# Windowed attention and a sticky mixture of experts: local scores in 64-row by 32-column tiles, and half of v spread on the chip

## The chip, the cores and the metric

The kernel runs on one core of a Trainium2 chip. The metric is the device time of the program in microseconds; lower is better. A core has five engines that run their own instruction streams: TensorE (PE; PEld is its weight loading), VectorE (DVE), ScalarE (ACT), GpSimd (POOL) and SyncE (SP), which here issues most of the loads.

## The reference

There are 8 batches, 8 heads of 64 dimensions, 512 local and 32 global positions. A global query attends to everything; a local query attends to the 32 global keys and to local keys at most 32 positions away.

```python
k_all = np.concatenate([k_g, k_l], axis=2)
v_all = np.concatenate([v_g, v_l], axis=2)
out_g = np.matmul(sm(scale * np.matmul(q_g, k_all.transpose(0, 1, 3, 2))), v_all)
s_ll = scale * np.matmul(q_l, k_l.transpose(0, 1, 3, 2))
mask = np.abs(pos[:, None] - pos[None, :]) <= 32
s_ll = np.where(mask, s_ll, -1000000000.0)
s_lg = scale * np.matmul(q_l, k_g.transpose(0, 1, 3, 2))
a_l = sm(np.concatenate([s_lg, s_ll], axis=-1))
out_l = np.matmul(a_l, np.concatenate([v_g, v_l], axis=2))
x = np.concatenate([out_g, out_l], axis=2)   # then (B, S, H * D)
...
# per token: an expert is chosen (fresh, or the previous token's), then
h = np.maximum(x[b, s] @ w1[e], 0.0)
out[b, s] = p[e] * (h @ w2[e])
```

## The kernel before

The kernel has two stages. The attention (class Attn) works in units: per batch, four local units, one for each pair of heads, and two global units, one for two pairs. Their order is l0, l1, g0, l2, g1, l3; 48 units in all. Each batch also computes its gate logits (f1, f2, f3) and stores its rows to a scratch tensor in DRAM (f4). The experts (class Moe) then gather rows by expert and multiply them; their first pieces start during the last attention units.

The schedule is written out by hand in Attn.run. In step s it issues: the load of q and k two pairs ahead and of v one pair ahead (SP's queue); prep, which GpSimd does, for the next pair; the transposes of the probabilities of unit s - 2 (l_t, g_t); the mask matmul of unit s (l_m); a wide piece of the gate work; the scores of unit s (l_s, g_s) and their maximum (l_max, g_max); a thin piece; the exponential; and the product with v of unit s - 2 (l_av, g_av). Scores use a ring of three PSUM banks, the products a ring of two. Small steps of routing (the generators that drip calls) go between VectorE's instructions.

A pair's 512 queries are 16 windows of 32. The two heads lie on partitions 0 to 63 and 64 to 127 of the loaded tile raw. Before, prep copies q into a block-diagonal tile qbd (32 columns per head and window, the other head's half zero) and the keys into a tile kx, which for two windows holds their local blocks and the global block side by side. One matmul per window (L246) takes 64 columns of qbd as weights over all 128 partitions and streams 128 keys: 16 a pair. Each f32 matmul shows in the trace as two instructions, each with its weight load. Two windows share a bank column block, one on output partitions 0 to 63, one on 64 to 127. The mask is added first by a matmul with the identity (L235). VectorE takes the maximum (L251), subtracts it out of PSUM (L253), ScalarE applies the exponential (L257). After a transpose (L263) and a copy (L265) the product with v (L279) runs in 32-column tiles, and VectorE divides (L282, L284, L287).

v comes from DRAM already spread: for each of the 16 windows the 128 rows that its probabilities meet (its own, its neighbours' and the global ones), 16 x 130 columns, 1040 KB a pair. The host lays inputs out in _layout; no time is counted for it.

f4 stores a batch's 512 rows with one DMA (L420) from ScalarE's queue, for the last two batches from SP's. The first steps clear the zero halves of qbd and kx (blank).

## Time and profile before

| quantity | value |
|---|---|
| median of 3 runs | 682.33 us (679.4 to 682.5) |
| the profiled execution | 682.57 us |
| its span | 680.8 us |
| TensorE busy | 651.2 us |
| VectorE busy | 430.1 us |
| ScalarE busy | 344.6 us |
| GpSimd busy | 205.8 us |
| DMA moved | 151.46 MB |
| granted TensorE clock | 0.992 |

The span runs from the first to the last instruction; the time of an execution has 1.8 us around it. A row of a group has: line, engine, operation, output <- inputs by the program's names, shapes, xcount | busy us, mean ns of one | idle us of the engine just before them, and what ended that. A row of the timeline has: start us, duration us, engine, line, operation, xcount [idle before]. A row of the waits has: who, waited for whom: us in total, times, longest.

### The profile page before, as it was taken

Reading aid. Unit: us, or ns where it says so; the run is one execution under the profiler, and the core shown is the slowest. Engines: PE = TensorE matmul, PEld = TensorE weight load, DVE = VectorE, ACT = ScalarE, POOL = GpSimd, SP = SyncE. Lnnn points to the kernel's source line nnn. Section 1 sums busy time; section 2 is a strip of 40 time slices with the busy share of each in tenths; the row PEclk is TensorE's granted clock in tenths of the full one; section 3 lists DMA queues with packets and bytes.
Section 4 is the critical chain, followed back from the end, with each engine's and each line's share of the span. In section 5 each row is a group of like instructions: output and inputs, shape, how many; then the busy total and the mean of one; then the engine's idle time right before and its main releaser. Section 6 shows DMA issues by size and latency. Waiting matters only on the chain.

```text
span 680.8 us, 18547 instructions
## 1 busy us (share of the span) xinstructions
PE 651.2 (96%) x7261; PEld 560.6 (82%) x7261; DVE 430.1 (63%) x1090; ACT 344.6 (51%) x620; POOL 205.8 (30%) x342
## 2 busy tenths in 40 slices
PE   8899999998999999999999999999999999999994
PEld 6688788786776879887889888889898989898893
DVE  7878687787987877976407545526363627265552
ACT  4465665664555764555317626334455326166543
POOL 7644344343662310033012313040304020133113
PEclk9999999999999999989999999999999999999997
DMA  8857978879585596867318566437374626175583
GB/s 321 350 202 265 322 253 333 306 260 345 206 317 201 194 344 214 294 199 235 117 41 293 201 252 201 148 101 272 88 274 139 218 67 243 54 277 185 182 288 99
DMA packets 43013, 151.46 MB, mean 222 GB/s; under 512 B 7965, under 2 KB 9245, under 8 KB 38688
## 3 DMA queue, kind: packets, MB, share of 16 engines
q1 hardware_dynamic: 32080, 120.42, 50.5%
q0 software_dynamic: 6960, 21.90, 9.8%
q10 hardware_dynamic: 3744, 6.63, 2.6%
q8 instruction: 78, 1.28, 0.8%
q14 instruction: 151, 1.24, 0.6%
HBM read 130.55 MB, written 19.69 MB: 221 GB/s over the span
## 4 chain that ended last, share of the span: by engine, by line
PE 81%; DVE 10%; issue 4%; POOL 2%; ACT 1%; DMA 1%; POOLq 0%; ACTq 0%; DVEq 0%
PE ps L1284 27%; PE ps L1296 23%; PE ps L246 7%; PE ps L263 4%; PE ps L279 4%; PE ps L1238 3%; PE ps L1301 2%; PE ps L355 2%; DVE wp L1191 2%; PE ps L342 2%; PE ps L299 2%; PE ps L331 2%; PE ps L370 1%; DVE pe L253 1%; DVE mx L251 1%
## 5 line engine op out<-in xcount | busy, mean ns | idle before, releaser
L1312 POOL DMA_INDIRECT out_dram<-y,tk x39 | 41.3, 1058 | 311.8 <-ACT y L1309 155.4
L1284 PE MATMUL ps<-wp,wp 128*128 128x256 f32 (+6 forms) x744 | 118.0, 318 | 0.0
L1284 PEld LDWEIGHTS ps<-wp,wp 128*128 128x128 f32 x744 | 112.0, 189 | 5.4 <-ACT wp L1240 0.4
L1296 PE MATMUL ps<-wp,wq 128*128 128x512 f32 x444 | 111.5, 398 | 0.5 <-DVE wq L1288 0.5
L1296 PEld LDWEIGHTS ps<-wp,wq 128*128 128x128 f32 x444 | 81.6, 188 | 17.8 <-ACT wq L1286 0.7
L1288 DVE SCALAR_TENSOR_TENSOR wq<-ps,wq 128x384 fp32r<-128x384 f32 (+4 forms) x120 | 44.9, 409 | 55.9 <-ACT wq L1286 49.8
L1286 ACT ACTIVATE wq<-ps 128x256 fp32r<-128x256 f32 (+6 forms) x88 | 39.4, 452 | 72.7 <-PE ps L1284 65.8
L190 POOL TENSOR_SCALAR_AFFINE_SELECT qbd<-raw 64x512 f32<-64x512 f32 x62 | 44.3, 715 | 97.3 <-PE ps L246 89.0
L1241 DVE TENSOR_TENSOR wp<-ps,wp 128x512 fp32r<-128x512 f32 x40 | 27.6, 691 | 71.5 <-ACT wp L1240 71.3
L246 PE MATMUL ps<-kx,qbd 128*64 128x128 f32 x1024 | 64.7, 276 | 3.7 <-issue 3.6
L246 PEld LDWEIGHTS ps<-kx,qbd 128*64 128x64 f32 x1024 | 55.4, 137 | 11.7 <-issue 9.1
L251 DVE TENSOR_REDUCE mx<-ps 128x4 f32<-128x512 f32 x64 | 43.8, 685 | 30.0 <-PE ps L246 28.8
L1309 ACT ACTIVATE y<-ps,pp 128x512 f32<-128x512 f32 x39 | 26.8, 687 | 66.4 <-PE ps L1296 60.2
L257 ACT ACTIVATE pe<-pe 128x512 f32<-128x512 f32 x64 | 40.8, 638 | 37.9 <-DVE pe L253 37.9
L1191 DVE TENSOR_TENSOR wp<-raw,wp 128x1024 fp32r<-128x1024 f32 x47 | 56.7, 1218 | 4.5 <-ACT wp L1178 4.3
L1224 POOL DMA_INDIRECT xa<-xs,idx x42 | 50.5, 1203 | 17.3 <-issue 11.1
L1240 ACT CAST wp<-ps 128x512 fp32r<-128x512 f32 x40 | 23.3, 586 | 55.5 <-PE ps L1238 55.5
L1178 ACT CAST wp<-raw 128x1024 fp32r<-128x1024 f32 x49 | 50.6, 1047 | 0.9 <-PE ps L342 0.6
L253 DVE TENSOR_TENSOR pe<-ps,mx 128x512 f32<-128x512 f32 x64 | 43.9, 686 | 1.0
L190 POOL TENSOR_SCALAR_AFFINE_SELECT kx<-raw 128x384 f32<-128x384 f32 (+3 forms) x127 | 42.8, 370 | 2.7 <-DMA raw<-in_qk_dram 0.6
L279 PEld LDWEIGHTS ps<-v,pt 128*32 128x32 f32 x2048 | 32.1, 110 | 11.4 <-issue 8.8
L265 ACT COPY pt<-ps 128x512 f32<-128x512 f32 x64 | 34.7, 599 | 10.8 <-PE ps L263 10.8
(284 smaller groups left out, 1183.0 us busy)
## 6 DMA issues: line engine op xcount, KB each, us to landing
raw<-in_w_dram SPq DMA_DIRECT2D x78, 512.0 KB
v<-in_vw_dram SPq DMA_DIRECT2D x32, 1040.0 KB
raw<-in_qk_dram SPq DMA_DIRECT2D x32, 528.0 KB
xa<-in_w_dram SPq DMA_DIRECT2D x26, 512.0 KB
xT<-in_w_dram SPq DMA_DIRECT2D x20, 512.0 KB
xs<-xa ACTq DMA_DIRECT2D x6, 1056.0 KB
xs<-xa SPq DMA_DIRECT2D x2, 1056.0 KB
qgb<-in_qg_dram SPq DMA_DIRECT2D x8, 128.0 KB
```

The source lines that it names most:

```text
L190: self.nc.gpsimd.affine_select(out=out, in_=in_, pattern=pat, compare_op=ALU.is_ge, fill=0.0, base=0, channel_multiplier=0)
L246: nc.tensor.matmul(sp[64 * t2:64 * t2 + 64, t], qbd[:, w], kf[:, f:f + P], start=False, stop=True, skip_group_check=True)
L251: nc.vector.tensor_reduce(out=mx, in_=st["sps"][hb], axis=AX.X, op=ALU.max)
L253: nc.vector.tensor_tensor(out=st["pe"][:, 4 * hb:4 * hb + 4], in0=st["sps"][hb], in1=mx.broadcast_to([P, 4, P]), op=ALU.subtract)
L279: nc.tensor.matmul(o[32 * w4:32 * w4 + 32, g, h], pt[:, 2 * g + w4 // 2, w4 % 2, h, :], v[:, w, h * (D + 1):(h + 1) * (D + 1)], start=True ...
L1178: (nc.vector.tensor_copy if dve else nc.scalar.copy)(out=hi, in_=raw)
L1191: (nc.gpsimd if pool else nc.vector).tensor_tensor(out=lo[:, f], in0=raw[:, f], in1=hi[:, f].bitcast(F32), op=ALU.subtract)
L1224: self.nc.gpsimd.indirect_dma_start(out=self.xr[j] if k == "early" else self.xr4[:, j], out_offset=None, in_=src, in_offset=bass.IndirectO ...
L1284: nc.tensor.matmul(ph, a[:, dc, fs], b_[:, dc, n0:n1], start=(n == 0), stop=(n == 11))
L1288: nc.vector.scalar_tensor_tensor(out=t, in0=ph[:, a - n0:b_ - n0], scalar=0.0, in1=hh[:, fc, a:b_].bitcast(F32), op0=ALU.max, op1=ALU.subt ...
L1296: nc.tensor.matmul(py, a[:, fc, js], b_[:, fs], start=(fc == 0 and k == 0), stop=(fc == 7 and k == 2))
L1312: sc = nc.gpsimd.indirect_dma_start(out=self.out, out_offset=bass.IndirectOffsetOnAxis(ap=self.g[1][:, j:j + 1], axis=0), in_=y, in_offset ...
```

## The change

- q is used as it lies. For each window and head one matmul takes 32 columns of q on that head's 64 partitions as weights and streams 128 keys on the same 64 partitions: 32 matmuls a pair on tiles of 64 rows by 32 columns, in place of 16 on 128 by 64. Scores of head h go to bank h. The mask is now two matmuls of 128 columns for each bank.
- k is loaded in blocks of 64 in an order PO, and prep writes one region of 28 blocks of 32 behind it, in the same tile: the global block, spread 14 times, and the local blocks 1 to 14. A pair's window reads two stretches of 64. qbd, kx and the clearing are gone.
- v is loaded for the eight even windows only (8 x 130 columns). The odd ones, which need the same rows except one neighbour, are written by GpSimd in two copies (prepv): 96 partitions x 1040, and 32 partitions x 910 from partitions 0 to 31 to 96 to 127.
- Each load of q and k or of v waits on SP until the last but one has landed (AHEAD = 2).
- A batch's row store is split in two; for the first six batches the second half is issued a step later, after the first exponential.
- The thin gate piece runs after the first product (after g_av, where there is none). The global scores are cut into 320 and 224 columns, with three exponentials in place of five.
- Buffers move: raw is wider, and the experts' row buffers xr, their output ring y and one weight buffer now lie in raw's upper part.

```diff
-GCH = [1, 4, 7, 10, 13, 14]
+GCH = [8, 2, 11, 5, 14, 0]
+PO = [0, 2, 3, 5, 6, 1, 4, 7]
+AHEAD = 2
...
+    def get(self, out, in_):
+        d = self.nc.sync.dma_start(out, in_)
+        if len(self.sent) >= AHEAD:
+            self.tc.add_manual_dep(d.ins, self.sent[-AHEAD].ins.name, mybir.DependencyInfo(mybir.DependencyClass.Sync, mybir.DependencyReason.DATA), reason="chain")
+        self.sent.append(d)
...
-        self.nc.sync.dma_start(t, self.qk[b, pr])
+        self.get(t[:, 0:33 * 32], self.qk[b, pr])
...
-        self.nc.sync.dma_start(v.rearrange("p w c -> p (w c)"), self.vw[b, pr])
+        self.get(v[:, 0:8].rearrange("p w c -> p (w c)"), self.vw[b, pr])
...
     def prep(self, u):
...
-            self.cp(qbd[0:64, :, 0, :], q[0:64], [[0, NW], [0, 32]])
-            self.cp(qbd[64:128, :, 1, :], q[64:128], [[0, NW], [0, 32]])
-        self.cp(kf[:, 1:5]...
-        self.cp(kf[:, 6:24]...
-        self.cp(kf[:, 24]...
-            self.cp(kx[:, 1:8, 2, :]...
+            self.cp(x[:, :, 0], g, [[0, 14], [0, 32]])
+            self.cp(x[:, :, 1], k[:, 1:15], [[0, 14], [0, 32]])
...
+    def prepv(self, u):
+        b, pr = u["u"]
+        v = self.cur[b]["v"][pr]
+        self.cp(v[0:96, 8:16], v[0:96, 0:8], [[0, 8], [0, VW]])
+        self.cp(v[96:128, 8:15], v[0:32, 1:8], [[0, 7], [0, VW]])
...
+        for sp in st["sps"]:
+            so = sp.rearrange("p t (k c) -> p t k c", c=32)
+            for par, mo in enumerate((so[:, 0:2, 1::2, :], so[:, 2:4, 0::3, :])):
+                nc.tensor.matmul(mo, self.cst.idb, self.mask[:, par], start=(par == 0), stop=False, skip_group_check=True)
...
-        for t in range(4):
-            for t2 in range(2):
-                w = 8 * hb + 2 * t + t2
-                f = 32 * (3 * (w // 2) + w % 2)
-                nc.tensor.matmul(sp[64 * t2:64 * t2 + 64, t], qbd[:, w], kf[:, f:f + P], start=False, stop=True, skip_group_check=True)
+        for t2 in range(2):
+            for par in range(2):
+                for w4 in range(4):
+                    for h in range(2):
+                        m = 4 * t2 + w4
+                        far = min(max(2 * m - 1, 1), 14) if par == 0 else min(2 * m + 2, 14)
+                        u0, u1 = 8 + PO.index(m), 16 + 2 * PO.index(far // 2) + far % 2
+                        d = slice(64 * h, 64 * h + 64)
+                        w = 2 * m + par
+                        nc.tensor.matmul(st["sps"][h][32 * w4:32 * w4 + 32, 2 * par + t2], q[d, 32 * w:32 * w + 32], ku[d, u0:u1 + 1:u1 - u0],
+                                         start=False, stop=True, skip_group_check=True)
...
-        q.dma_start(self.xs[r0:r0 + 4 * P].rearrange("(t p) r -> p t r", p=P), xa)
+        q.dma_start(out[:, 0:2], xa[:, 0:2])
+        if b < B - 2:
+            self.rows.append((out[:, 2:4], xa[:, 2:4]))
+        else:
+            q.dma_start(out[:, 2:4], xa[:, 2:4])
...
+                self.prepv(nx)
...
-                self.l_s(nx, 0)
+                self.l_s(nx)
                 self.l_max(nx, 0)
-                self.l_s(nx, 1)
                 self.l_max(nx, 1)
...
-            fpiece(thin)
             if nl:
                 self.l_exp(nx, 0)
             else:
                 self.g_exp(nx)
+            for _ in range(old):
+                nc.scalar.dma_start(*self.rows.pop(0))
             if sl:
                 self.l_av(st, 0)
+                fpiece(thin)
                 self.l_av(st, 1)
...
-        self.xr = [buf.tile([P, ROW], F32, name=f"xr{j}") for j in range(2)]
+        self.xr = [raw.t[j][:, 1024:1024 + ROW] for j in range(2)]
...
-    raw = ring(buf, [P, 32 * 33], F32, "raw", 4)
+    raw = ring(buf, [P, 1536 + ROW], F32, "raw", 4)
```

## The prediction

> **What bounds the kernel now.** I read the page first: the busy shares, the chain that ended last and the costliest groups.

> ```profile
> span 680.8 us, 18547 instructions
> PE 651.2 (96%) x7261; PEld 560.6 (82%) x7261; DVE 430.1 (63%) x1090; ACT 344.6 (51%) x620; POOL 205.8 (30%) x342
> PE 81%; DVE 10%; issue 4%; POOL 2%; ACT 1%; DMA 1%; POOLq 0%; ACTq 0%; DVEq 0%
> L246 PE MATMUL ps<-kx,qbd 128*64 128x128 f32 x1024 | 64.7, 276 | 3.7 <-issue 3.6
> ```

> TensorE is busy 96% of the span and 81% of the chain. The local scores (L246) are 64.7 us of that, so a microsecond off TensorE there is a microsecond off the end until another engine is in the way. Next I cut the attention into stretches of one batch's length (six units) by the windows view. Its columns are stretch, length, busy us of each engine, clock, DMA share, GB/s.

> ```profile
> 23.30:51.20 27.90, 25.55 (x586) 20.92 (x585) 21.86 (x85) 15.63 (x38) 12.48 (x28) 1.00 0.66 247
> 78.80:104.60 25.80, 25.71 (x590) 21.41 (x589) 21.32 (x73) 15.68 (x36) 11.03 (x24) 1.00 0.83 290
> 104.60:130.80 26.20, 25.85 (x589) 21.40 (x587) 20.94 (x73) 15.87 (x38) 11.05 (x24) 1.00 0.86 303
> 158.00:189.40 31.40, 28.91 (x616) 23.27 (x615) 25.87 (x91) 14.51 (x32) 16.59 (x33) 1.00 0.69 247
> 189.40:224.00 34.60, 31.77 (x656) 25.57 (x655) 26.82 (x99) 20.99 (x49) 15.94 (x29) 1.00 0.76 275
> 224.00:320.00 96.00, 91.66 (x773) 78.94 (x772) 76.69 (x191) 55.90 (x88) 21.41 (x23) 0.98 0.74 243
> ```

> A middle batch is TensorE alone: 25.71 of 25.80 us busy, at full clock. But VectorE is busy 21.32 of the same 25.80, and DMA 83 to 86%. After 224 us come the experts, which the change touches only by where buffers lie. Last, the timeline of two units, to see who waits for whom.

> ```profile
> 104.56 0.38 PE L235 MATMUL ps<-mask,idb 128*128 128x256 bf16 x2
> 105.31 1.97 PE L246 MATMUL ps<-kx,qbd 128*64 128x128 f32 x32
> 106.45 0.69 DVE L251 TENSOR_REDUCE mx<-ps 128x4 f32<-128x512 f32 x1 [1.84 <-PE ps L246]
> 107.17 0.69 DVE L253 TENSOR_TENSOR pe<-ps,mx 128x512 f32<-128x512 f32 x1
> 107.20 1.12 PE L279 MATMUL ps<-v,pt 128*32 128x65 f32 x64
> 108.26 0.88 PE L331 MATMUL ps<-idf,pg 128*128 128x128 f32 x6
> 108.97 0.38 PE L235 MATMUL ps<-mask,idb 128*128 128x256 bf16 x2
> 110.14 0.15 DVE L282 TENSOR_SCALAR rs<-ps 128x4 f32<-128x4 f32 x1
> 110.32 0.18 DVE L284 RECIPROCAL rs<-rs 128x4 f32<-128x4 f32 x1
> 110.54 0.42 DVE L287 TENSOR_TENSOR xa<-ps,rs 128x256 f32<-128x256 f32 x1
> DVE mx L251 <- PE ps L246: 27.7, 21, 2.2
> L279 PE MATMUL ps<-v,pt 128*32 128x65 f32 x2048 | 37.7, 221 | 2.3 <-issue 1.5 <-DVE rv L894 0.3 <-DVE xa L287 0.2
> ```

> TensorE goes from one group to the next without a hole. VectorE is the one that waits, for the first half of the scores, 1.3 us each time (27.7 over 21 waits).

> **The local scores, the main term.** Before, a pair's scores are 32 passes (16 f32 matmuls, two instructions each) on 128-row by 64-column tiles; two such tiles stand side by side. 32 passes take 1.97 us, a single one 0.276, so they start (1.97 - 0.276) / 31 = 54.6 ns apart. With two tiles running together that is 109 ns per pass on a tile, 0.85 ns a column. L279 shows the same with four 32-column tiles: (1.12 - 0.221) / 63 = 14.3 ns apart, 57 ns per pass on a tile, 0.88 ns for each of 65 columns. So column tiles overlap in full, twofold and fourfold, both passes of a matmul included.

> After, there are 64 passes of 128 columns on eight tiles (two row halves, one per head, by four column strips). Nothing in this trace runs a row-split tile. If all eight overlap, starts are 109 / 8 = 13.7 ns apart and the block takes 63 x 13.7 + 276 = 1.14 us: 0.83 us saved a pair, 26.6 us over 32 pairs. If only the four column strips overlap, starts are 27.3 ns apart and the block takes 1.99 us: nothing gained. If neither did better than the present 54.6 ns, the block would take 3.7 us: a loss of 56 us. I take 13.7 ns, since L279 already issues at 14.3 with as many columns open and the two heads write different banks.

> [...]

> **Mask.** Four matmuls of 128 columns replace two of 256.

> ```profile
> 9.12 0.27 PE L235 MATMUL ps<-mask,idb 128*128 128x256 bf16 x1 [1.40 <-DVE pe L253]
> L1023 PE MATMUL ps<-oe,o x21: 167/168/182, 201.8 to 202.5; 128*128 128x12 bf16 x21
> ```

> The two of 256 at 104.56 come 0.38 less the 0.27 of a single one, 0.11 us, apart, 0.22 a pair. L1023 issues 21 bf16 matmuls, with full weights, in 0.7 us, 33 ns each, so 55 ns for half the columns is not held up by the weights. I take 0; the other end, 0.11 us for each of four, is +0.22 x 32 = 7 us.

> **VectorE, who is late next.** A batch needs 25.71 - 4 x 0.83 = 22.4 us of TensorE against VectorE's 21.3. Also, scores now come by head, both banks complete only at the block's end, so the first reduction no longer starts halfway. VectorE's work for a unit after that end is four operations of 0.69 and two evacuations of about 0.75 (0.15, 0.18 and 0.42), 4.24 us. The unit that starts at 104.56 lasts 4.41 to the next mask and would last 3.58: a deficit of 0.66 us. Units beside global ones have slack and catch up. TensorE needs the first bank back for the mask after 1.12 of L279 and 0.88 of L331, 2.0 us from the block's end; VectorE frees it after 1.4, so some 0.6 us of lag costs nothing. I take 0.8 us a batch, 6.4 in all; the ends are 0 and half of what was saved (1.7 a batch, 13 us).

> **GpSimd.** Rows of its copies, all at L190:

> ```profile
> L190 POOL TENSOR_SCALAR_AFFINE_SELECT qbd<-raw 64x512 f32<-64x512 f32 x62 | 44.3, 715 | 97.3 <-PE ps L246 89.0 <-DMA raw<-in_qk_dram 4.1 <-DMA xr<-xs,idx 2.1
> L190 POOL TENSOR_SCALAR_AFFINE_SELECT kx<-raw 128x384 f32<-128x384 f32 x32 | 17.8, 555 | 0.0
> L190 POOL TENSOR_SCALAR_AFFINE_SELECT kx<-raw 128x224 f32<-128x224 f32 x31 | 12.9, 416 | 0.0
> L190 POOL TENSOR_SCALAR_AFFINE_SELECT kx<-raw 128x128 f32<-128x128 f32 x32 | 9.5, 295 | 2.7 <-DMA raw<-in_qk_dram 0.6
> L190 POOL TENSOR_SCALAR_AFFINE_SELECT kx<-raw 128x32 f32<-128x32 f32 x32 | 6.9, 214 | 0.0
> ```

> A pair costs 2 x 0.715 + 0.555 + 0.416 + 0.295 + 0.214 = 2.91 us. After: two key copies of 448 columns, 0.555 + 64 x 0.87 ns = 0.61 each; two v copies of 1040 and 910 columns, at 1.09 ns a column (715 - 295 over 384) 1.29 and 1.15; together 3.66. A batch rises from 11.0 to 14.0 us of 23, and GpSimd was waiting for TensorE for 89 us, so this is hidden: 0. Behind the v copy, which waits for its load, stand the next pair's key copies, the setup and ranking steps and the gathers; scores and products that need the copies come two units later. If the v copies ran at half that speed GpSimd would need 24 us a batch and set the pace, at +1 us a batch or 8 in all.

> **Loads and stores.**

> ```profile
> v<-in_vw_dram SPq DMA_DIRECT2D x32, 1040.0 KB
> raw<-in_qk_dram SPq DMA_DIRECT2D x32, 528.0 KB
> 121.76 0.37 ACTq L420 DMA_DIRECT2D xs<-xa  x1
> ```

> v drops from 1040 to 520 KB a pair: 32 x 520 KB, 16.6 MB less. A middle batch moves 290 GB/s x 25.8 us = 7.5 MB; it would move 5.4 in 23.2, 232 GB/s, a share near 0.66. Each load waits on SP for the last but one; behind it on SP stand the query loads, the global rows' stores and at the end the weight loads; GpSimd waits for those loads. 303 GB/s at a share of 0.86 is 352 at full share, 1.5 us a load; a pair's two loads have 5.8 us. I take 0. Six half stores more on ScalarE (15.9 of 26.2 us busy) and two fewer exponentials a global unit are hidden by its slack; the thin pieces, moved behind the first exponential and product, feed work one unit later: 0. Uncovered they would cost at most a store issue each, 6 x 0.4 us.

> **Supply of instructions.** TensorE also stands still where the profile shows no wait:

> ```profile
> q8 instruction: 78, 1.28, 0.8%
> 32.03 0.87 PE L246 MATMUL ps<-kx,qbd 128*64 128x128 f32 x11 [1.64 <-issue]
> 77.53 0.43 PE L342 MATMUL ps<-v,ptg 128*32 128x65 f32 x16 [1.50 <-issue]
> 165.81 0.76 PE L246 MATMUL ps<-kx,qbd 128*64 128x128 f32 x9 [1.95 <-issue]
> ```

> These fall in stretches with heavy loads, and instructions arrive by DMA too. The change eases the loads but adds 32 matmul and 32 weight-load instructions a pair. I take 0, between -5 (these three gone) and the loss of the third rival.

> **Start.** The clearing of block-diagonal buffers goes from VectorE, so the wait of 1.40 us at 9.12 can; the first v copies then queue on GpSimd ahead of the next keys. 0, between -1.4 and +2.

> Sum: 682.6 (the profiled execution, 680.8 of span and 1.8 around it; 0.2 over the median 682.33) - 26.6 + 6.4 = 662.4 us.

> **The rivals.** First, VectorE or GpSimd takes back half or more of the gain: 26.6 - 13 - 8 leaves 6 us, 26.6 - 13 leaves 14; 669 to 677, centre 673. For it speaks VectorE at 21.3 against 22.4, against it the 0.6 us of lag that is free. [...]

> Second, the row halves do not overlap, and the change does not do what it says: blocks of 1.99 us, 683, with the mask's end up to 690. For it: no row-split tile is in the trace. Against: strips overlap without loss.

> Third, slower: TensorE runs out of instructions. A batch now executes 590 + 589 in 25.8 us, 45.7 a us. After, it has 4 x 64 more and 16 for the masks, 1451, in 23.2 us, 62.5 a us. Below 1451 / 25.8 = 56 a us the batch is slower than before; at 54 it takes 26.9, 1.1 us more, 691. For it the holes above; against it the lower DMA share, and 128 instructions in L279's 1.12 us.

> Fourth, more is gained: no VectorE loss, the three holes and the 1.4 at the start gone: 682.6 - 26.6 - 5.1 - 1.4 = 649.5.

> **How the numbers follow.** Likeliest (652 to 669) 0.56; VectorE or GpSimd 0.13; the floor 0.03; no overlap 0.10; supply 0.10; more gained 0.08. A change of 0.5%, 3.4 us, is about what a measurement of this kernel can tell. Faster: 0.56 + 0.13 + 0.03 + 0.08 = 0.80, less 0.01 for the edge of the floor: 0.79. No overlap splits into 0.06 same and 0.04 slower; with the edge, same 0.07; slower 0.10 + 0.04 = 0.14. The range 650 to 682 leaves out the supply case, most of no overlap and part of the last.

> **What would show it.** L246's successor: 64 matmuls in 1.1 to 1.2 us, right; near 2.0, the second rival. A batch of 23 to 24 us with VectorE over 0.9 busy: right. Waits of TensorE's mask or products for L253 and L287 above 1 us a batch: the first rival; issue holes above the present ones: the third. DMA share near 0.66, GpSimd 14 us a batch. What makes the prediction wrong is mainly the untested row split, then the supply.

## The result: 1.1% slower, and where the profile shows it

The changed kernel takes 687.97 us (median of 4 runs, 687.05 to 689.35), the kernel before beside it 680.87 us (4 runs, 679.36 to 682.5): a ratio of 1.0106, interval 1.0069 to 1.0142. The forecast was 662 us and faster.

The profiled executions are 687.05 us now and 682.57 before, so they show 4.5 of the 7.1 us between the medians. All of it lies in the attention: its last score block ends at 224.1 us before and at 229.3 us after, and what follows takes 456.7 and 456.1 us. The page of the changed kernel, the lines that answer to those shown of before:

```profile
span 685.3 us, 20668 instructions
PE 633.9 (92%) x8349; PEld 540.1 (79%) x8349; DVE 431.8 (63%) x1087; ACT 337.7 (49%) x588; POOL 225.1 (33%) x279
q8 instruction: 85, 1.39, 0.8%
L251 PE MATMUL ps<-raw 64*32 64x128 f32 x2048 | 41.5, 282 | 8.8 <-issue 8.6
L200 POOL TENSOR_SCALAR_AFFINE_SELECT v<-v 96x1040 f32<-96x1040 f32 x64 | 66.9, 1045 | 51.4 <-DMA v<-in_vw_dram 31.2
v<-in_vw_dram SPq DMA_DIRECT2D x32, 520.0 KB
```

TensorE lost 17.3 us of busy time (651.2 to 633.9) and the span grew all the same: work went and idle time came. The score row went from 64.7 to 41.5 us of busy time, its idle time from 3.7 to 8.8, and nearly all of that is "issue", time with no wait that the profile shows. The same stretches as before (stretch, length, busy us of each engine, clock, DMA share, GB/s), and one of 3.5 us:

```profile
23.30:51.20 27.90, 23.82 (x715) 18.59 (x713) 20.73 (x79) 14.21 (x31) 16.70 (x20) 0.94 0.55 169
78.80:104.60 25.80, 22.63 (x710) 17.93 (x689) 23.06 (x72) 13.85 (x31) 13.36 (x16) 1.00 0.67 214
104.60:130.80 26.20, 22.18 (x664) 17.50 (x661) 20.07 (x65) 14.23 (x32) 11.24 (x14) 0.93 0.66 211
111.50:115.00 3.50, 3.50 (x110) 2.94 (x100) 1.95 (x5) 0.21 (x1) 3.15 (x4) 0.52 0.57 191
158.00:189.40 31.40, 27.02 (x796) 21.69 (x788) 25.99 (x90) 16.52 (x37) 11.46 (x15) 1.00 0.62 199
```

The DMA share has fallen to 0.66 as forecast, but TensorE is now idle for 3 to 4 us of each 26. The clock column, 1.00 in these stretches before, reads 0.94 and 0.93 in two of them: TensorE ran at half clock for a while. The row from 111.50 is one such piece, clock 0.52. The timeline (start, length, engine, instruction, and in brackets the idle time before it and what ended it) shows a good unit and the two kinds of hole:

```profile
104.37 0.39 PE L236 MATMUL ps<-mask,idb 128*128 128x128 bf16 x4
...
105.13 1.16 PE L251 MATMUL ps<-raw 64*32 64x128 f32 x64
106.21 1.12 PE L285 MATMUL ps<-v,pt 128*32 128x65 f32 x64
106.32 0.69 DVE L257 TENSOR_REDUCE mx<-ps 128x4 f32<-128x512 f32 x1 [1.86 <-PE ps L251]
...
108.14 2.15 POOL L200 TENSOR_SCALAR_AFFINE_SELECT v<-v 96x1040 f32<-96x1040 f32 x2 [5.18 <-PE ps L334]
108.25 1.04 DVE L755 TENSOR_TENSOR leq<-L,lm 128x40 f32<-128x40 f32 x1
108.74 0.41 PE L251 MATMUL ps<-raw 64*32 64x128 f32 x5
...
111.35 1.74 PE L251 MATMUL ps<-raw 64*32 64x128 f32 x59 [2.20 <-issue]
...
166.46 2.15 POOL L200 TENSOR_SCALAR_AFFINE_SELECT v<-v 96x1040 f32<-96x1040 f32 x2 [6.00 <-PE ps L334]
167.72 0.91 DVE L765 TENSOR_TENSOR lvm<-sk,lvm 128x5 f32<-128x5 f32 x1
...
170.86 0.90 PE L345 MATMUL ps<-v,ptg 128*32 128x65 f32 x48 [2.63 <-DVE rs L288]
```

At 105.13 a score block takes 1.16 us: this part works. At 108.74 a block gets 5 passes out, stands still for 2.20 us with nothing to wait for, and does the other 59 at half clock (1.74 us). At 166.46 two v copies run on GpSimd; beside them VectorE takes 0.91 us for 5 columns, and then TensorE waits 2.63 us for VectorE. The view of waits over the attention (0 to 224 us; idle us of the waiting engine, number, longest) names the same two. It also names an engine, GpSimd, that waits for loads; from 5 us on, no hole of TensorE over 0.2 us in this trace ends with GpSimd:

```profile
POOL v L200 <- DMA v<-in_vw_dram: 31.2, 19, 4.9
POOL raw L200 <- DMA raw<-in_qk_dram: 29.4, 16, 5.3
PEld ps L251 <- issue: 14.8, 32, 2.5
PE ps L251 <- issue: 8.5, 5, 2.2
PE ps L345 <- DVE rs L288: 6.6, 4, 2.6
```

**An account of the attention.** For each kernel I took the holes of more than 0.2 us in TensorE (neither a matmul nor a weight load running; a wait for a semaphore that TensorE's queue records as an instruction of its own counts as hole) from 5 us to the end of the last score block, and sorted them by what ended them. A hole is "instruction" when the next instruction starts 0.9 to 1.7 us after a 16 KB packet of the instruction queue (q8 above) has landed and no engine has just released it. All holes counted so lie at one place of TensorE's stream: 193 or, seldom, 194 instructions past a multiple of 256, in the order of the trace. A hole is VectorE's, ScalarE's or GpSimd's when the next instruction, or the queue's wait just ahead of it, waits on a semaphore of that engine and starts 28 to 105 ns after an instruction of that engine ended. "Half" is the time at clock 0.5, which always came behind a hole, in pieces of 3.4 us or of two or three times that. "Work" is the end, less the holes, less half of "half"; that last term is an estimate, since TensorE need not have been the bound all through such a piece. Worked out from the traces, in us (number of instruction holes in brackets):

```
kernel                       end    instr.     VectorE ScalarE GpSimd other half  work
before                       224.1   7.5 (8)     1.9    1.0    0      1.5    0    212.1
after                        229.3  14.2 (12)   16.8    1.5    0      0.4  10.2   191.3
e1_no_chain                  241.7  25.2 (15)   14.9    1.0    0      0.8  17.1   191.2
e2_chain_one                 265.8   3.8 (4)    42.2    0.5    8.5    2.0  51.2   183.1
e3_small_copies              231.3  14.4 (14)   13.4    0.9    1.4    0.4  20.5   190.5
e4_whole_v                   250.1  33.0 (23)    8.2    1.4    0      3.2  27.3   190.6
e5_scores_alone              244.6  34.0 (23)    7.2    0.5    0      0    23.9   190.9
e6_after_more_instr          287.3  51.1 (30)    3.5    1.0    0      0    41.0   211.3
e7_before_more_instr         269.9  37.7 (23)    0.5    1.3    0      0    13.7   223.7
e8_small_loads               221.7   2.2 (3)    23.4    1.3    0      0    10.2   189.7
e9_half_loads                220.6  10.7 (15)   14.7    0.8    0      0     0     194.4
e10_small_loads_no_copies    207.4   1.6 (2)    12.1    1.3    0      0     3.4   190.7
e11_half_loads_small_copies  225.7   9.9 (11)   14.6    3.6    0.7    0    13.7   190.0
e12_quarter_loads            232.3  11.2 (14)   16.7    5.2    0      0    10.2   194.1
e13_copy_on_scalar           229.4   7.6 (8)    15.6   12.7    0      0     3.4   191.9
e14_half_loads_four          225.4   9.9 (14)   17.1    4.7    0      0     6.8   190.2
e15_before_part_loads        232.0   0.9 (1)     2.1   16.3    0.4    0    10.2   207.1
```

From before to after: work -20.8; VectorE's holes +14.9; instruction holes +6.7; half clock +5.1; ScalarE +0.5; other -1.1. That is +5.3, and the trace has +5.2.

Of VectorE's 16.8 us, 10.8 are in front of product matmuls (L345 6.9, L285 3.9; 0.5 before). They wait for a bank of the ring of two that VectorE empties by its division (L288, L290, L293): 9.3 of the 10.8 us end within 0.15 us of the end of L293. The mask, which waits for a score bank, has 2.5 us (1.4 before). A hole of 0.96 us that ends at 93.82 shows how VectorE comes late:

```profile
91.13 2.15 POOL L200 TENSOR_SCALAR_AFFINE_SELECT v<-v 96x1040 f32<-96x1040 f32 x2 [0.91 <-DMA v<-in_vw_dram]
92.24 0.18 DVE L290 RECIPROCAL rs<-rs 128x4 f32<-128x4 f32 x1
92.45 0.84 DVE L791 TENSOR_TENSOR gx<-lpr,lsu 32x8 f32<-32x8 f32 x1
93.33 0.42 DVE L293 TENSOR_TENSOR xa<-ps,rs 128x256 f32<-128x256 f32 x1
```

A routing step (L791) stands between two steps of the division. Beside the v copies it takes 0.84 us, 0.16 where no copy runs, and the product's bank comes free that much later.

Each row of the table is one profiled execution. Its time can lie several us from the median of its kernel: e7 8.0 us below, e13 3.6, e2 3.4 and e9 3.1 below, e1 2.9 above; e8 and e10 ran once. So differences of a few us between rows are not told apart by them. The expectations below were written with a count that took the recorded waits of TensorE's queue for work; in it VectorE's holes are 13.6 us in the changed kernel, 16.5 in e8 and 14.1 in e9.

### The profile page after: what moved, and what is told of

The parts are those of the page before. It is cut to its first block, busy times and chain, and to the rows that moved or that the text cites. A ratio compares the mean times of both kernels' runs of the same rounds, so it can differ in the third digit from the quotient of the medians.

```text
span 685.3 us, 20668 instructions
## 1 busy us (share of the span) xinstructions
PE 633.9 (92%) x8349; PEld 540.1 (79%) x8349; DVE 431.8 (63%) x1087; ACT 337.7 (49%) x588; POOL 225.1 (33%) x279
## 4 chain that ended last, share of the span: by engine, by line
PE 56%; DVE 5%; issue 2%; ACT 1%; POOL 0%; POOLq 0%; ACTq 0%; DVEq 0%
PE ps L1298 27%; PE ps L1310 23%; PE ps L1252 2%; PE ps L1315 2%; DVE wp L1205 1%; DVE wq L1205 1%; DVE hl L1302 0%; DVE xT L1021 0%; PE ps L1036 0%; POOL xa L1238 0%; DVE o L937 0%; DVE xl L1255 0%; DVE xT L1023 0%; PE ps L358 0%; POOLq L1460 0%
## 5 line engine op out<-in xcount | busy, mean ns | idle before, releaser
L1326 POOL DMA_INDIRECT out_dram<-raw,tk x39 | 41.1, 1053 | 311.0 <-ACT raw L1323 168.0
L200 POOL TENSOR_SCALAR_AFFINE_SELECT v<-v 96x1040 f32<-96x1040 f32 x64 | 66.9, 1045 | 51.4 <-DMA v<-in_vw_dram 31.2
L1323 ACT ACTIVATE raw<-ps,pp 128x512 f32<-128x512 f32 x39 | 26.8, 688 | 66.8 <-PE ps L1310 60.6
L1238 POOL DMA_INDIRECT xa<-xs,idx x42 | 51.0, 1214 | 16.7 <-issue 10.9
L285 PEld LDWEIGHTS ps<-v,pt 128*32 128x32 f32 x2048 | 33.5, 109 | 21.4 <-issue 10.2
L251 PE MATMUL ps<-raw 64*32 64x128 f32 x2048 | 41.5, 282 | 8.8 <-issue 8.6
L285 PE MATMUL ps<-v,pt 128*32 128x65 f32 x2048 | 41.1, 222 | 8.8 <-issue 3.7
L200 POOL TENSOR_SCALAR_AFFINE_SELECT raw<-raw 128x448 f32<-128x448 f32 x62 | 39.0, 655 | 30.1 <-DMA raw<-in_qk_dram 29.4
L251 PEld LDWEIGHTS ps<-raw 64*32 64x32 f32 x2048 | 30.4, 109 | 16.3 <-issue 15.5
## 6 DMA issues: line engine op xcount, KB each, us to landing
raw<-in_qk_dram SPq DMA_DIRECT2D x32, 528.0 KB
xs<-xa ACTq DMA_DIRECT2D x12, 528.0 KB
xs<-xa SPq DMA_DIRECT2D x4, 528.0 KB
```

Source lines behind the costliest of these rows:

```text
L200: self.nc.gpsimd.affine_select(out=out, in_=in_, pattern=pat, compare_op=ALU.is_ge, fill=0.0, base=0, channel_multiplier=0)
L251: nc.tensor.matmul(st["sps"][h][32 * w4:32 * w4 + 32, 2 * par + t2], q[d, 32 * w:32 * w + 32], ku[d, u0:u1 + 1:u1 - u0], start=False, stop ...
L285: nc.tensor.matmul(o[32 * w4:32 * w4 + 32, g, h], st["pts"][h][:, 2 * par + hb, c0:c0 + 32], v[:, 8 * par + m, h * (D + 1):(h + 1) * (D + ...
L1238: self.nc.gpsimd.indirect_dma_start(out=self.xr[j] if k == "early" else self.xr4[:, j], out_offset=None, in_=src, in_offset=bass.IndirectO ...
L1326: sc = nc.gpsimd.indirect_dma_start(out=self.out, out_offset=bass.IndirectOffsetOnAxis(ap=self.g[1][:, j:j + 1], axis=0), in_=y, in_offset ...
```

## The experiments

Four theories of what gave the gain back are tested; the letters are those of the expectations. S: the supply of instructions, TensorE waits for a fetch that stands behind data loads. C: the chain, a load that waits for the last but one comes late. G: GpSimd's v copies slow VectorE down. V: VectorE itself is late, by its own work. Ratios are against the kernel before on the same chip.

**The chain of loads.** First without it, then tighter.

```diff
-AHEAD = 2
+AHEAD = 99        # e1_no_chain
+AHEAD = 1         # e2_chain_one
```

> Only the chain is taken out: loads no longer wait for the last but one. Theory S (TensorE runs out of instructions, because there are more of them per microsecond and their fetch waits behind loads): bursts of loads come back, fetches wait longer, the holes with no wait grow from about 21 us; 690 to 696 us. Theory C (the chain makes loads late: GpSimd waited 61 us for DMA): these waits shrink below 20 us and 4 to 8 us come back; 680 to 684. Theory G (GpSimd's v copies hold VectorE's small two-input operations): no change, 686 to 690.

697.58 us, ratio 1.0213 (1.0141 to 1.0286), against 1.0106 (1.0069 to 1.0142) with the chain: slower, though the intervals touch. Its waits over the attention:

```profile
POOL v L200 <- DMA v<-in_vw_dram: 52.6, 18, 5.1
PE ps L251 <- issue: 11.3, 7, 2.6
PE ps L285 <- issue: 11.0, 6, 3.2
```

Instruction holes rise from 14.2 to 25.2 us, and GpSimd waits longer for v, not shorter. So C falls as a cost of the change: at two loads the chain helps.

> One load in flight instead of two. Theory S: a fetch finds at most one load ahead of it, holes fall by half; 680 to 685 us as long as loads arrive in time. Theory C: GpSimd's waits for loads double; 693 to 700. Theory G: 686 to 690.

727.01 us, 1.0686 (1.0635 to 1.0737), beyond every range expected. The instruction holes fall to 3.8 us, so S holds; but now data is late: GpSimd waits 61.7 us for v and 44.6 for keys (31.2 and 29.4 in the changed kernel). VectorE's holes are 42.2 us and half clock 51.2; that they hang on the late data is likely, and not traced. The chain trades one lateness for the other: of the three settings run, two loads is the best.

**The v copies in eight pieces.** G said that a VectorE operation is held until the end of the copy it meets.

```diff
-        self.cp(v[0:96, 8:16], v[0:96, 0:8], [[0, 8], [0, VW]])
-        self.cp(v[96:128, 8:15], v[0:32, 1:8], [[0, 7], [0, VW]])
+        for j in range(0, 8, 2):
+            self.cp(v[0:96, 8 + j:10 + j], v[0:96, j:j + 2], [[0, 2], [0, VW]])
+            n = min(2, 7 - j)
+            self.cp(v[96:128, 8 + j:8 + j + n], v[0:32, 1 + j:1 + j + n], [[0, n], [0, VW]])
```

> The two v copies of a pair (1040 and 910 columns, about 1.05 us each) are cut into eight of 130 to 260 columns; GpSimd works longer in all. Theory G: VectorE's two-input operations wait for a copy's end, so their excess (about 11 us in the attention, 2 before) falls to a third and 4 to 8 us come back; 680 to 684 us. Theories S and C: 686 to 690.

690.9 us, 1.0161 (1.0106 to 1.0216): no better. One small VectorE operation with two inputs, in the groups of the kernel before, the changed one and this one (count, busy us, mean ns):

```profile
L742 DVE TENSOR_TENSOR leq<-L,lm 128x40 f32<-128x40 f32 x7 | 1.4, 201 | 0.1
```

```profile
L755 DVE TENSOR_TENSOR leq<-L,lm 128x40 f32<-128x40 f32 x6 | 3.8, 625 | 0.1
```

```profile
L200 POOL TENSOR_SCALAR_AFFINE_SELECT v<-v 96x260 f32<-96x260 f32 x248 | 97.5, 393 | 42.4 <-DMA v<-in_vw_dram 25.8 <-PE ps L336 4.0 <-PE ps L287 0.3
L757 DVE TENSOR_TENSOR leq<-L,lm 128x40 f32<-128x40 f32 x6 | 1.4, 226 | 0.1
```

201 ns before, 625 after, 226 with short copies. Summed over VectorE's operations of the attention with two inputs, none of them in PSUM, the time above the usual length (the median of the same operation over eight of the traces) is 4.0 us before, 10.0 after and 2.1 here. So the lengthening is real and comes from long copies. But VectorE's holes fall only from 16.8 to 13.4 us, while GpSimd's own time for v rises from 66.9 to 97.5 us (248 x 393 ns) and half clock rises. That long copies stretch VectorE's operations, as G says, is shown; that this is the whole of VectorE's lateness is not.

**No copies, v whole by DMA, and the scores alone.** e4 lays out all 16 sets of v on the host and loads them; e5 takes away the chain and the split stores too. What e5 still has of the change is the new score tiles with their keys, the moved gate pieces, the other cut of the global scores and the moved buffers.

```diff
-        self.get(v[:, 0:8].rearrange("p w c -> p (w c)"), self.vw[b, pr])
+        self.get(v.rearrange("p w c -> p (w c)"), self.vw[b, pr])
-                self.prepv(nx)
# e5 besides:
-AHEAD = 2
+AHEAD = 99
+        q.dma_start(out, xa)      # rows in one part
```

> v is loaded whole again (1040 KB a pair), no v copies on GpSimd; score tiles, chain and split stores stay. Theory S: DMA share back above 0.8 and a fetch waits longer; 690 to 697 us. Theory C: loads twice as long on the chain, later still; 690 to 697. Theory G: VectorE is free of the copies; 680 to 684.

706.96 us, 1.0357 (1.0292 to 1.0423). VectorE's holes halve (16.8 to 8.2), but with 16.6 MB more to load instruction holes go from 14.2 to 33.0 us. How much of the halving is the copies is not told apart here, since TensorE's longer stops also give VectorE time. Its waits:

```profile
POOL raw L200 <- DMA raw<-in_qk_dram: 131.0, 22, 10.6
PE ps L251 <- issue: 12.2, 10, 1.8
```

> The score tiles alone: v loaded whole, no v copies, no chain, row stores whole. Theory S: loads as heavy and as unordered as before with 23% more instructions in the attention; holes of the instruction kind 30 us or more; 700 to 712 us. Theories G and C: without copies and chain the 17 us that TensorE saves show; 664 to 675.

705.41 us, 1.0423 (1.0367 to 1.0479). The new score tiles, without the other loads, make the kernel 4.2% slower: work falls from 212.1 to 190.9 us, and 34.0 us of instruction holes and 23.9 us at half clock take it back. The other parts of the change (half the v load, the chain, the split stores) recover some 3 points of the 4.2.

**More instructions for the same work.** e6 splits each score matmul by columns in the changed kernel, e7 each product matmul in the kernel before; neither changes a load.

```diff
# e6_after_more_instr: each 128-column score matmul as two of 64
+                        for c in range(2):
+                            u = u1 if c else u0
+                            nc.tensor.matmul(st["sps"][h][32 * w4:32 * w4 + 32, 2 * par + t2, 64 * c:64 * c + 64], q[d, 32 * w:32 * w + 32], ku[d, u], ...
# e7_before_more_instr: each 65-column product matmul of the kernel before as 33 and 32
+                    for a, z in ((0, 33), (33, 65)):
```

> The changed kernel with each score matmul cut into two of 64 columns: the same columns streamed, 64 more matmul and 64 more weight-load instructions a pair, nothing else. Theory S (instruction supply): a batch executes 1963 instead of 1451 instructions; if one batch of instructions (256) takes about 4.2 us to arrive, that is 61 a us and 32 us a batch; 715 to 735 us. Theories C and G (loads, v copies): the score block grows from 1.16 to at most 1.3 us; 688 to 693.

744.99 us, 1.0964 (1.0929 to 1.0998), more than any theory expected. The trace of the changed kernel has, on average, 1.70 us from TensorE's 200th instruction past a multiple of 256 to the start of a packet and 1.00 us to its landing, and at the instruction holes 1.42 us more until TensorE goes on: 4.1 us, beside the 4.2 of theory S. Of the attention's 58 us, instruction holes bring 36.9 (14.2 to 51.1 us), half clock 15.4 and work 20.0; VectorE's holes shrink by 13.3. The timeline has a block of twice the instructions, and a hole:

```profile
60.23 1.86 PE L253 MATMUL ps<-raw 64*32 64x64 f32 x128
...
87.49 0.93 PE L253 MATMUL ps<-raw 64*32 64x64 f32 x52 [1.59 <-issue]
```

Here my expectation missed: I had the block at 1.3 us at most. 128 passes of 64 columns take 1.86 us, 14.5 ns each at most, where 64 passes of 128 columns start 13.9 ns apart: half the columns did not bring the starts closer by more than a little. So about 0.7 us a block, 22 us in all, is TensorE's own rate of issue, and this run prices the supply only together with it.

> The kernel before with each product matmul cut into one of 33 and one of 32 columns: nothing changed but 64 more matmul and 64 more weight-load instructions a pair (1691 a batch instead of 1179). Theory S: holes without a wait grow although scores, loads and GpSimd are as before; 695 to 715 us. Theories C and G: only the product block is a little longer (1.12 to 1.3 us at most); 681 to 688.

738.79 us, 1.0913 (1.0872 to 1.0954), again more than expected. With no change to the scores, TensorE's instruction holes rise from 7.5 to 37.7 us.

```profile
110.49 1.50 PE L280 MATMUL ps<-v,pt 128*32 128x33 f32 x128
```

128 passes in 1.50 us are at most 11.7 ns apart: 0.38 us a block of TensorE's own, 12 us over 32 pairs; the holes are 30 us on top, and half clock some 7. So S needs nothing of the change's own but its instructions: the kernel before already lived near that edge.

**Loads taken away.** e8 loads an eighth of keys and v after the first four pairs; e10 leaves out the v copies of those pairs as well.

```diff
+        n = 33 * 32 if NP * b + pr < 4 else 132         # columns of queries and keys
+        n = 8 if NP * b + pr < 4 else 1                 # sets of v
# e10 besides, in prepv:
+        if NP * b + pr >= 4:
+            return
```

> The changed kernel, but from the fifth pair on only an eighth of each load is made; the rest of the tiles keeps older pairs' numbers, so the result is not the reference's, and what the experts do after the attention differs; only the attention's length is read (the last scores end at 229 us in the changed kernel, 224 before). Theory S: a fetch finds no load ahead of it, holes without a wait fall below 3 us after the fifth pair, the attention ends at 203 to 212. Theory G: VectorE's excess of 11 us stays and the attention ends at 222 to 230. Theory C: GpSimd's waits for loads vanish, the attention ends at 215 to 222, holes without a wait stay.

The attention ends at 221.7 us, 7.6 before the changed kernel. Instruction holes go from 14.2 to 2.2: nearly all of them hung on the data loads. That is what S expected, but not its end of 203 to 212: VectorE's holes grow from 16.8 to 23.4 us, and the three pieces at half clock all come behind those. What one limit gives back, the other partly takes.

> e8 (small loads) and also no v copies from the fifth pair on; the result is not the reference's, and only the attention's length is read. In e8 holes of the instruction kind were gone (2 us) but 16.5 us of holes ended with VectorE, and the attention ended at 222. Theory G (GpSimd's v copies hold VectorE's small operations, 7 us in e8): the excess falls to 2 us, VectorE's holes below 9, the attention ends at 211 to 216. Theory V (VectorE has no slack left once the scores are short and both banks complete late, copies or not): VectorE's holes stay at 13 to 17 us and the attention ends at 218 to 222.

207.4 us: without loads and copies the attention ends 16.7 us before that of the kernel before, of the 20.2 that the forecast's sum had, and better than G or V expected. VectorE's holes halve (23.4 to 12.1 us): the copies are worth 11.3 us there, and another 3.4 of half clock. 12.1 us stay without any copy, so part of G and part of V hold. (The experts then work on another routing, so for e8 and e10 only the attention is compared.) The stretch from 80 to 140 us of five kernels, in the order before, after, e4, e8, e10:

```profile
80.00:140.00 60.00, 59.30 (x1367) 49.60 (x1362) 49.56 (x167) 36.17 (x83) 26.65 (x58) 1.00 0.87 311
```

```profile
80.00:140.00 60.00, 51.41 (x1550) 40.72 (x1539) 49.11 (x159) 32.70 (x71) 28.66 (x34) 0.97 0.66 213
```

```profile
80.00:140.00 60.00, 48.27 (x1362) 37.51 (x1363) 38.18 (x137) 27.84 (x61) 8.76 (x14) 0.91 0.66 228
```

```profile
80.00:140.00 60.00, 53.65 (x1601) 42.61 (x1600) 51.60 (x158) 33.23 (x73) 31.47 (x39) 0.97 0.24 70
```

```profile
80.00:140.00 60.00, 57.58 (x1820) 45.38 (x1821) 50.74 (x180) 37.65 (x84) 12.52 (x20) 1.00 0.27 81
```

Instructions of TensorE (matmuls and weight loads) a microsecond: 45.5 before, 51.5 after, 45.4 in e4, 53.4 in e8, 60.7 in e10. The forecast wanted 62.5, and e10 nearly has it: TensorE and VectorE can go at that pace. With loads and copies in place they do not, and the changed kernel's 51.5 lie below the 56 under which the forecast's third rival had a batch slower than before. VectorE, 0.82 busy in the changed kernel here, is not full where it is late.

**Can the loads be kept and the fetches let through?** The same bytes in smaller pieces, with as many or fewer bytes under way at once.

```diff
# e9_half_loads: AHEAD = 3, every load in two pieces
+        for k in (0, 528):
+            self.get(t[:, k:k + 528], self.qk[b, pr][:, k:k + 528])
+        for k in (0, 4):
+            self.get(v[:, k:k + 4].rearrange("p w c -> p (w c)"), self.vw[b, pr][:, k * VW:(k + 4) * VW])
# e12_quarter_loads: AHEAD = 5, every load in four pieces
# e14_half_loads_four: e9 with AHEAD = 4
# e11_half_loads_small_copies: e9 with the copies of e3
```

> The changed kernel with each load cut in two, and each half waiting for the last but two (three halves, about 0.8 MB, in flight instead of 1.05). Theory S: a fetch waits less (1.2 to 1.4 us instead of 1.7), holes fall; 678 to 685 us. Theory C: loads are no earlier; 686 to 692. Theory G: 686 to 690.

681.51 us (6 runs), 1.0070 (1.0027 to 1.0112). The estimate lies below the changed kernel's 1.0106, but the intervals overlap. In its profile the instruction holes are 10.7 us, many and mostly short, and no hole was followed by half clock; that execution, the fastest of the six, ended its attention 3.5 us before the kernel before. The waits:

```profile
POOL v L202 <- DMA v<-in_vw_dram: 45.8, 21, 5.5
PEld ps L253 <- issue: 11.2, 33, 1.5
```

> Each load in four, each waiting for the one five before it (0.66 MB in flight instead of e9's 0.8). Theory S: a fetch waits less still than e9's 1.64 us, instruction holes 5 to 8 us; 0.997 to 1.006 of the kernel before. If the shorter queue makes loads late instead: GpSimd's waits for loads grow above e9's 69 us; 1.010 or more.

693.48 us, 1.0179 (1.0082 to 1.0276): quarters do not go on where halves began. Instruction holes are 11.2 us, ScalarE's 5.2. The loads did not come later: GpSimd waits 61.5 us for them, 69.4 in e9. Why it is slower stays open.

> e9 with four halves in flight (1.05 MB, as in the changed kernel, but in smaller pieces). Theory S by bytes in flight: as the changed kernel, instruction holes 13 to 15 us; 1.010 to 1.016 of the kernel before. If it is the pieces' size and not the bytes that counts: as e9, 1.002 to 1.010.

682.77 us, 1.0060 (1.0039 to 1.0082), the same as e9 with a third more bytes under way. Instruction holes are 9.9 us. Mean wait of a fetch for its packet to begin, counted from TensorE's 200th instruction past a multiple of 256: 2.07 us before, 1.70 after, 1.64 in e9, 1.57 in e14, 2.44 in e4, 1.17 in e8, 1.05 in e10. It follows how much is loaded, and pieces of half the size did little to it.

> e9 (half loads, three in flight; 681.5 against 678.5 on that chip) and the v copies in eight small pieces. Theory S with G: VectorE's holes fall from 14 to 8 us beside e9's 9 us of instruction holes; 0.5 to 1% under e9, so 0.993 to 1.002 of the kernel before. Theory S with V: as e9, 1.003 to 1.010 of the kernel before.

683.36 us, 1.0044 (1.0016 to 1.0072), the smallest ratio of any version with the new tiles, not told apart from e9 and e14. Still slower than before.

**The second v copy on ScalarE**, on top of e9, to leave VectorE half as much of it on GpSimd beside it.

```diff
-        self.cp(v[96:128, 8:15], v[0:32, 1:8], [[0, 7], [0, VW]])
+        self.nc.scalar.copy(out=v[96:128, 8:15], in_=v[0:32, 1:8])     # after l_exp(nx, 0)
```

> e9 (half loads) with the 32-partition v copy moved to ScalarE, behind the unit's first exponential; GpSimd keeps the 96-partition one. Theory G (copies on GpSimd hold VectorE): half of the copy time on GpSimd gone, VectorE's excess from 9 to about 5 us and its holes from 14 to 9 or 10; 0.993 to 1.002 of the kernel before. Theory V (no slack on VectorE whatever the copies): as e9 or slower, ScalarE's exponentials come 1 us later; 1.005 to 1.015.

692.06 us, 1.0226 (1.0178 to 1.0273). Inconclusive for G: the copy delays ScalarE itself, whose holes go from 0.8 to 12.7 us, and the lengthening of VectorE's small operations did not fall (10.0 us, 8.1 in e9).

```profile
PEld ps L291 <- ACT pt L277: 10.4, 17, 3.3
```

**The kernel before with loads in pieces**, to see whether the piecing alone would help it.

```diff
+            if len(self.sent) >= 4: ...     # each load waits for the last but three
+        for k in (0, 528): ...              # queries and keys in two pieces
+        for k in range(0, NW, 4): ...       # v in four
```

> The kernel before with its loads in pieces of about 0.26 MB, each waiting for the one four before it (about 1.05 MB in flight); scores, v and stores as before. Theory S: its 7.5 us of instruction holes fall to 3 or 4; 0.992 to 0.997 of the kernel before. If the chain makes its larger loads late instead: GpSimd and the products wait for DMA; 1.005 to 1.03.

693.3 us, 1.0230 (1.0186 to 1.0274). Its instruction holes go from 7.5 to 0.9 us, the gain that S sees, and it is lost to holes that end with ScalarE (16.3 us) and to half clock (10.2). GpSimd waits for loads, and ScalarE's idle time in the longest of these holes ends, by the profile, with a load (the waits, and a row of the timeline):

```profile
PE ps L379 <- ACT xT L365: 12.2, 4, 7.7
POOL qbd L199 <- DMA raw<-in_qk_dram: 30.6, 10, 3.9
```

```profile
75.37 1.07 ACT L274 COPY pt<-ps 128x512 f32<-128x512 f32 x2 [8.03 <-DMA raw<-in_qk_dram]
```

No version run here beats the kernel before.

## Why the prediction was wrong, point by point

- **Local scores, -26.6.** Right in its mechanism: 64 passes on 64-row by 32-column tiles take 1.16 us against 1.14 forecast, (1.16 - 0.282) / 63 = 13.9 ns apart, so row halves and column strips all run together. The second rival, with blocks of 1.99 us, is out. No run shows the floor under the distance of matmul starts that has 0.03 among the chances, and an edge of 0.01: L279's starts were 14.3 ns apart before, and those of the new score tiles are 13.9. Per block that is 0.81 us, 25.9 us in all; work at full clock fell by 20.8. Where the other 5 us stay I have not traced; holes of less than 0.2 us count as work.
- **Mask, 0.** Right: four matmuls in 0.39 us, two took 0.38.
- **GpSimd, 0 for its own time.** Busy 13.36 us in the stretch from 78.80, with v copies of 1.05 us on average (forecast 1.29 and 1.15): right. Wrong in what it does to its neighbour (0.20 us of a VectorE operation became up to 1.04 beside a v copy), which the step did not price.
- **VectorE, +6.4.** The first of two steps that failed. Its holes rose by 14.9 us, over the bound of 13. The step priced one wait, the mask's for a score bank with 0.6 us of lag free; that wait has 2.5 us, 1.4 before. It put no price on the products, which wait for the division to empty one of two banks, and there are 10.8 us. The cause I gave (both banks complete only at the block's end) was not tested alone; that VectorE is late by its own work at this pace is shown by the 12.1 us that stay without copies (e10). The copies are the rest, 11.3 us with small loads (e8 against e10). The stretched operations explain a part of that at most, since e3 removed 7.9 us of stretch and only 3.4 us of holes; how the copies cost the rest is open.
- **Loads and stores, 0.** The volume and the share of 0.66 came true. The chain, which I took for nothing, is worth some 7 us for the better (ratios 1.0213 without it and 1.0106 with it), and costs 39 us when it is one load tighter (1.0686).
- **Supply of instructions, 0.** The second step that failed. I saw the three holes and the third rival, and left the middle at nothing because the loads would ease. Fetches did come a little sooner (2.07 to 1.70 us), but there are more of them (36 packets before, 44 after in the attention) and TensorE uses one up in less time (224.1 / 36 = 6.2 us before, 229.3 / 44 = 5.2 after, holes included). Holes went from 7.5 to 14.2 us. e8 shows that they hang on the loads, e7 that more instructions alone bring them.
- **Not in the prediction at all: the clock.** TensorE ran at half speed in three pieces of 3.4 us, about 5 us of loss by the estimate above: two behind instruction holes (1.68 and 2.20 us), one behind a hole of 0.89 us that ended with VectorE. Before, there was no such piece in the attention.
- **The sum.** The forecast had the attention 20.2 us shorter, and it became 5.2 longer. Of the 25.4 between, VectorE is 8.5, the supply 6.7, work that did not go 5.8 and the clock 5.1, with -0.6 for the rest.
- **The rivals.** The third, at a chance of 0.10 and 691 us, came nearest to the time (688), though the first's mechanism brought more: neither alone would have made the kernel slower. Against work of -20.8, VectorE alone leaves 5.9 us of gain, and supply with all of the half clock 9.0. I gave each a chance as if one excluded the other; together they decide the sign, and e10, without the loads and the copies, gains 16.7 us.

## What to carry to other kernels

Before packing TensorE denser, count the instructions a microsecond that it will need and look for issue holes that are already in the trace: here faster tiles moved the limit in part to the fetch of instructions (holes of 7.5 us before, 14.2 after), which hung on the data loads (2.2 us with an eighth of them). Where another engine has little slack, price each bank that it gives back, not only the one that comes first. Costs that are each smaller than the gain add up, so rivals that can hold at once are summed, and not only weighed one by one. A copy moved to GpSimd is not free because GpSimd has time: look at what VectorE does beside it (its holes went from 23.4 to 12.1 us without the copies, e8 against e10).
